# One reading of w1 between the second and the third pass of a decode gradient kernel

## The chip, the cores and the metric

The kernel runs on one core of one Trainium2 chip. The metric is the device time of one execution in microseconds (us). One execution was recorded by the hardware profiler, and all times of single instructions below are from that record.

## The reference, cut to what matters

A small network for one token is run forwards and backwards. Attention block A reads a cache of keys and values (4 groups, 65536 positions, 128 wide, bf16); block B is a dense layer, and both are applied twice with the same weights:

```python
def _B_ref(x, w1, b1, w2, b2):
    h = jnp.einsum("bsd,df->bsf", x, w1) + b1      # w1: 1024 x 3584
    r = jnp.where(h > 0, h, 0)
    return jnp.einsum("bsf,fd->bsd", r * r, w2) + b2

x = x + _A_ref(_layernorm(x), k_cache, v_cache, wq, wo)   # first A
x = x + _B_ref(_layernorm(x), w1, b1, w2, b2)             # first B
x = x + _A_ref(_layernorm(x), k_cache, v_cache, wq, wo)   # second A
x = x + _B_ref(_layernorm(x), w1, b1, w2, b2)             # second B
# returned: x and the gradients by x, k_cache, v_cache, wq, wo, w1, b1, w2, b2
```

With `n` the normalised input of the second B and `g` the incoming gradient, the part that matters here is `h = n w1 + b1`, then `dh = 2 relu(h) (g w2^T)`, then `dn = dh w1^T`. The first product needs columns of w1 as stationary operands, the last one needs w1 turned.

## The kernel before, in words

The kernel goes over the cache four times: pass 1 and pass 2 are the two attention blocks forwards, pass 3 and pass 4 are them backwards. Between passes stand dense stages for the projections, the layer normalisation and block B. This text is about the dense stage between pass 2 and pass 3.

All large loads go to one SBUF tile, `arena`, cut into 20 slots of 1 MB (128 partitions x 4096 bf16). A planner in Python (`Slot`, `take_one`, `take_pair`, `FREE`) decides while the program is built which slot each load takes. Eight of the slots hold softmax weights of the passes (planes), and seven hold blocks of V that pass 2 keeps for pass 3, already turned. So the dense stage has five slots. The loads are issued by SyncE in one queue in the order of the program (`kv8`, L352 for one slot and L357 for a pair; `slabs`, L449, for weights). A load into a slot waits until the last reader of its old content is done, and whatever stands behind it in the queue waits as well.

Within the passes the order of TensorE (PE), VectorE (DVE) and ScalarE (ACT) is as written. In the dense stages a scheduler may mix neighbouring steps when the program is built. Each engine then runs its own list in order.

The steps of the dense stage before:

- `g_wo`: the last group's rows of wo are multiplied with the attention output, 64 matmuls of 64 columns (`g_mv`, L506), and added to `x3` (L908). The two loads were issued during pass 2.
- `ln_fwd`: the layer normalisation, two tiny matmuls (L212), DVE steps (L221 to L234) and one square root on ACT (L229). It ends with `L4["nb"]`.
- `g_w1`: w1 is read as 8 slabs of 128 rows x 3584 columns (896 KB each). Each slab gives 28 matmuls of 18 columns (L506); `h` is complete after the last slab. `ffn_act` then makes relu, square and their bf16 form.
- L1659: `dh4`, the gradient by h, from `dg4` (made between pass 1 and 2) and relu(h).
- `Rows` with `mix=True`: w1 is read a second time in the same slabs. A piece of 8 blocks of a slab is either turned on PE (L669), copied from PSUM by DVE or ACT (`evac`, L164 and L161) and multiplied with `dh4` (L701), or multiplied and summed on DVE alone (L660). A cost model (`load`) chooses per piece.
- `fin_dx3`: `ln_bwd` (L239 to L249) and `dx3` (L1655).
- `Rows` with `inplace=True`: 1024 rows of wo (two loads of 1 MB) are turned on PE (L669, 64 transposes), copied back into their slots, and multiplied with `dx3` (L701, 64 matmuls). `dO_finish` (L933 to L947) makes of it what pass 3 needs first; L933 is the first instruction after the last of these matmuls.

Pass 3 (`attn_bwd3`) turns V (L1201), multiplies it with the output gradient (L1221), and 13 steps later multiplies blocks of K (L1246). The kept blocks of V go first, and the first blocks of K are loaded in the dense stage as its slots come free. In the background of pass 3, `g_dO` reads rows of wo for the next group (multiplied on DVE, L585).

Of the kernel before, what the change touches and what calls it, by code (L numbers as in the profile page):

```python
# [10 lines left out]
BF = mybir.dt.bfloat16  # L11
F32 = mybir.dt.float32
ACTF = mybir.ActivationFunctionType
ALU = mybir.AluOpType
# [6 lines left out]
def kernel(  # L21
# [66 lines left out]
    def ps_tr(shape=None, dtype=BF):  # L88
        return PS["pool"].tile(shape or [P, 8, P], dtype, name="ps_tr", tag="tr", bufs=2 if PS["pass4"] else 3)

    def ps_sc(shape, dtype=F32):
        return PS["pool"].tile(shape, dtype, name="ps_sc", tag="sc", bufs=1 if PS["pass4"] else 2)
# [122 lines left out]
    def ln_fwd(x, name):  # L215
        s = tmp.tile([P, 1], F32, name="ln_s")
        nc.vector.reduce_sum(out=s[:], in_=x[:], axis=AX.X)
        mean = bcast_sum(s[:], 1, mean=True)
        xc = tmp.tile([P, DC], F32, name="ln_xc")
        negmean = tmp.tile([P, 1], F32, name="ln_negmean")  # L220
        nc.vector.tensor_scalar(out=negmean[:], in0=mean[:], scalar1=-1.0, scalar2=None, op0=ALU.mult)  # L221
        nc.vector.tensor_scalar(out=xc[:], in0=x[:], scalar1=negmean[:, 0:1], scalar2=None, op0=ALU.add)
        sq = tmp.tile([P, DC], F32, name="ln_sq")
        ss = tmp.tile([P, 1], F32, name="ln_ss")
        nc.vector.tensor_tensor(out=sq[:], in0=xc[:], in1=xc[:], op=ALU.mult)
        nc.vector.reduce_sum(out=ss[:], in_=sq[:], axis=AX.X)
        var = bcast_sum(ss[:], 1, mean=True)
        rstd = vec.tile([P, 1], F32, name=name + "_rstd")
        nc.scalar.activation(out=rstd[:], in_=var[:], func=ACTF.Sqrt, bias=eps_t[:], scale=1.0)  # L229
        nc.vector.reciprocal(out=rstd[:], in_=rstd[:])  # L230
        n = vec.tile([P, DC], F32, name=name + "_n")
        nc.vector.tensor_scalar(out=n[:], in0=xc[:], scalar1=rstd[:, 0:1], scalar2=None, op0=ALU.mult)
        nb = vec.tile([P, DC], BF, name=name + "_nb")
        nc.vector.tensor_copy(out=nb[:], in_=n[:])  # L234
        return n, nb, rstd

    def ln_bwd(dn, n, rstd):
        st = tmp.tile([P, 2], F32, name="lnb_st")
        nc.vector.reduce_sum(out=st[:, 0:1], in_=dn, axis=AX.X)  # L239
        pr = tmp.tile([P, DC], F32, name="lnb_pr")  # L240
        nc.vector.tensor_tensor(out=pr[:], in0=dn, in1=n[:], op=ALU.mult)
        nc.vector.reduce_sum(out=st[:, 1:2], in_=pr[:], axis=AX.X)
        tot = bcast_sum(st[:], 2, mean=True)
        negm = tmp.tile([P, 2], F32, name="lnb_negm")
        nc.vector.tensor_scalar(out=negm[:], in0=tot[:], scalar1=-1.0, scalar2=None, op0=ALU.mult)
        t = tmp.tile([P, DC], F32, name="lnb_t")
        nc.vector.scalar_tensor_tensor(out=t[:], in0=n[:], scalar=negm[:, 1:2], in1=dn, op0=ALU.mult, op1=ALU.add)  # L247
        dx = tmp.tile([P, DC], F32, name="lnb_dx")
        nc.vector.tensor_scalar(out=dx[:], in0=t[:], scalar1=negm[:, 0:1], scalar2=rstd[:, 0:1], op0=ALU.add, op1=ALU.mult)  # L249
        return dx  # L250
# [175 lines left out]
    def rows_of(W):  # L426
        return W.rearrange("(kc p) n -> p kc n", p=P)
# [50 lines left out]
    def wo_slabs(g, ahead=1):  # L478
        v = rows_of(A_wo)
        return slabs("s_wo", lambda k, kn: v[:, g * R + k:g * R + k + kn, :], R, 4, 1024, ahead, True)  # L480
# [6 lines left out]
    def w1_slabs(ahead=1):  # L487
        v = rows_of(B_w1)
        return slabs("s_w1", lambda k, kn: v[:, k:k + kn, :], DC, 1, F, ahead)
# [109 lines left out]
    class Rows:  # L599
# [147 lines left out]
        def run(self):  # L747
            self.fill()
            first = self.queue[0][0] if self.queue else None
            while first is not None and first["inplace"] and self.queue and self.queue[0][0] is first:  # L750
                self.back()
            self.fill()
            while self.queue:
                self.back()
                self.fill()
# [150 lines left out]
    def g_wo(L, xacc, g, ps=ps_bg, it=None):  # L906
        def fin(p):
            nc.vector.tensor_tensor(out=xacc[:], in0=xacc[:], in1=p, op=ALU.add)  # L908
        if it is not None:
            yield from g_mv(it, R, 8, lambda kc: L["oTb"][:, g * R + kc:g * R + kc + 1], ps, fin)  # L910
            return
        each = tmp.tile([P, R, 8], BF, name="run_each", bufs=1)
        nc.vector.tensor_tensor(out=each[:, :, :], in0=L["oTb"][:, gsl(g)].unsqueeze(2).to_broadcast([P, R, 8]),
                                in1=eighth[:, :].unsqueeze(1).to_broadcast([P, R, 8]), op=ALU.mult)
        yield
        pt = ps_mv([P, R, 8])
        nc.tensor.matmul(pt[:, :, :].rearrange("p r k -> p (r k)"), lhsT=to_runs[:, :, :].rearrange("p a b -> p (a b)"),
                         rhs=each[:, :, :].rearrange("p r k -> p (r k)"), start=True, stop=True)
        yield
        own = tmp.tile([P, 8, R], F32, name="run_own", bufs=1)  # L920
        nc.vector.tensor_tensor(out=own[:, :, :], in0=pt[:, :, :].rearrange("p r k -> p k r"),
                                in1=M8[:, :].unsqueeze(1).to_broadcast([P, 8, R]), op=ALU.mult)
        oruns = tmp.tile([P, 8], F32, name="run_o")
        nc.vector.tensor_reduce(out=oruns[:], in_=own[:, :, :], axis=AX.X, op=ALU.add)
        orunb = tmp.tile([P, 8], BF, name="run_ob")
        nc.vector.tensor_copy(out=orunb[:], in_=oruns[:])
        yield
        yield from g_mv(wo_runs(g), R, 8, lambda kc: orunb[:, kc:kc + 1], ps, fin)


    def dO_finish(L, g):
        def fin(y):
            nc.vector.tensor_copy(out=L["dOT"][:, gsl(g)], in_=y)  # L933
            prod = tmp.tile([P, R], F32, name="dlt_prod")
            nc.vector.tensor_tensor(out=prod[:], in0=L["dOT"][:, gsl(g)], in1=L["oT"][:, gsl(g)], op=ALU.mult)
            yield
            pd = ps_mv([33, R], F32)
            nc.tensor.matmul(pd[:, :], lhsT=ones_f[:, 0:33], rhs=prod[:, :], start=True, stop=True)
            yield
            negd = tmp.tile([33, R], F32, name="negd")  # L940
            nc.vector.tensor_scalar(out=negd[:], in0=pd[:], scalar1=-1.0, scalar2=None, op0=ALU.mult)
            hi = tmp.tile([33, R], BF, name="negd_hi")
            nc.vector.tensor_copy(out=hi[:], in_=negd[:])
            lo = tmp.tile([33, R], BF, name="negd_lo")
            nc.vector.tensor_tensor(out=lo[:], in0=negd[:], in1=hi[:], op=ALU.subtract)
            nc.vector.tensor_copy(out=L["nd2"][0:1, gsl(g)], in_=hi[0:1, :])
            nc.vector.tensor_copy(out=L["nd2"][32:33, gsl(g)], in_=lo[32:33, :])  # L947
        return fin
# [619 lines left out]
    def g_w1(L, ps, pre=None, it=None):  # L1568
        def fin(p):
            L["r"], L["g"], L["gb"] = ffn_act(p, L["name"])  # L1570
        yield from g_mv(it or w1_slabs()[0], DC, FC, lambda kc: L["nb"][:, kc:kc + 1], ps, fin, pre=pre, cols=f_cols)
# [37 lines left out]
    L2["n"], L2["nb"], L2["rstd"] = ln_fwd(x1, "L2")  # L1609
    run(g_w1(L2, ps_mv))  # L1610
    x2 = vec.tile([P, DC], F32, name="x2")
    dg4 = vec.tile([P, FC], F32, name="dg4")
    rows = Rows(DENSE["pool"])

    def fin_dg4(y):
        nc.vector.tensor_copy(out=dg4[:], in_=y)
    dgjob = rows.job(FC, DC, lambda: gx[:], fin_dg4, mix=True, vbc=gxbc)

    def side(kc, slab):
# [23 lines left out]

    reset_load()
    dst = open_dense("dense23")
    run(g_wo(L3, x3, lastg[1], ps_mv, PRE["wo3"]))
    L4 = dict(name="L4")
    L4["n"], L4["nb"], L4["rstd"] = ln_fwd(x3, "L4")
    rows = Rows(DENSE["pool"])
    dh4 = vec.tile([P, FC], F32, name="dh4")  # L1650
    dx3 = vec.tile([P, DC], F32, name="dx3")

    def fin_dx3(y):
        dxn = ln_bwd(y, L4["n"], L4["rstd"])
        nc.vector.tensor_tensor(out=dx3[:], in0=gx[:], in1=dxn[:], op=ALU.add)  # L1655
    rows.add(w1_slabs()[0], DC, FC, lambda: dh4[:], fin_dx3, cols=f_cols, mix=True)
    rows.add(wo_slabs(firstg[2])[0], R, DC, lambda: dx3[:], dO_finish(L3, firstg[2]), inplace=True)
    run(g_w1(L4, ps_mv, pre=rows.fill))
    nc.vector.scalar_tensor_tensor(out=dh4[:], in0=dg4[:], scalar=2.0, in1=L4["r"][:], op0=ALU.mult, op1=ALU.mult)  # L1659
    rows.run()  # L1660
    dst.close()

# [143 lines left out]
```

## Time and profile before

| what | value |
|---|---|
| device time, three runs | 1979.23, 1986.36, 1986.77 us; median 1986.36 us |
| profiled execution | span 1985.4 us from first to last instruction; the median of the runs is 0.96 us above it |
| busy, share of the span | PE 81%, DVE 59%, ACT 53%, GpSimd 7% |
| HBM | 624.96 MB read, 165.69 MB written, 398 GB/s over the span |
| DMA issues of w1 in the whole kernel | 32 of 896 KB, 7.5 us median from issue to landing |
| granted PE clock, mean | 0.905 of full speed |
| `arena` loads of w1 in this dense stage | 16, issued from 739.9 to 791.9 us of the span |

How to read it: the share of busy time is an average over stages with different limits. In a window of the trace, "DMA share" is the mean busy share of the core's 16 DMA engines, and "PEclk" is the clock that was granted to PE, 1.00 being full speed. A PE row with "x64" is 64 matmuls in a row, so its length over 64 is the pace; PEld rows are the loads of the stationary operands that go with them. SPq rows are issues of loads.

### The profile page before, as it was taken

To read this page: it belongs to the slowest core of one execution; us is meant where nothing else is said; L and a number is where in the kernel's file an instruction comes from. 1 tells how busy PE (TensorE), PEld (TensorE's weight loads), DVE (VectorE), ACT (ScalarE), POOL (GpSimd) and SP (SyncE) were. 2 spreads that over 40 slices of the span, in tenths; PEclk is the share of its full clock that TensorE was granted. 3 is DMA by queue.
4 is the path that set the end of the run, shared out by engine and by line. 5 is a ranking of instruction groups with operands and counts; after the bars stand their busy time and mean duration, and the time that the engine had idled before them with its cause. 6 is when DMAs were issued, how large, how long until landed. Compare 5 with 4: busy or idle time off the path is not lost. (4 is left out here: it accounts for less than half of the span.)

```text
span 1985.4 us, 67093 instructions
## 1 busy us (share of the span) xinstructions
PE 1614.0 (81%) x30228; PEld 1317.7 (66%) x30228; DVE 1174.4 (59%) x2426; ACT 1043.6 (53%) x1608; POOL 142.6 (7%) x332
## 2 busy tenths in 40 slices
PE   6878787687877877787877888887889898788897
PEld 6878777677777877786776886554556465455554
DVE  5645455255555543544544566877687586758666
ACT  3444344154344453534453455766678586657666
POOL 0000000000000000000000001111111111111211
PEclk9999899699999997998989999999899798879978
DMA  9999999999999998899999988999999999999996
GB/s 389 423 422 422 423 425 400 394 400 420 425 419 424 425 405 310 359 421 420 421 422 421 411 304 307 406 425 404 397 424 424 425 425 411 361 424 424 425 377 256
DMA packets 101037, 794.98 MB, mean 400 GB/s; under 512 B 9472, under 2 KB 9486, under 8 KB 37134
## 3 DMA queue, kind: packets, MB, share of 16 engines
q1 hardware_dynamic: 76670, 624.99, 76.6%
q0 software_dynamic: 24080, 165.70, 20.1%
q8 instruction: 236, 3.87, 0.8%
q14 instruction: 51, 0.42, 0.1%
HBM read 624.96 MB, written 165.69 MB: 398 GB/s over the span
## 5 line engine op out<-in xcount | busy, mean ns | idle before, releaser
L164 DVE COPY kt<-ps_tr 128x1024 bf16<-128x1024 bf16 x724 | 497.4, 689 | 431.0 <-PE ps_tr L1009 248.5
L161 ACT CAST arena<-ps_gg 128x1024 bf16<-128x1024 f32 x457 | 446.0, 1013 | 226.7 <-PE ps_gg L1393 140.2
L1009 PE MATMUL ps_tr<-ident_b,arena 128*128 128x128 bf16 x3840 | 310.4, 226 | 44.7 <-DMA arena<-in_A_k_cache_dram 30.7
L164 DVE CAST arena<-ps_gg 128x1024 bf16<-128x1024 f32 (+2 forms) x186 | 222.5, 1196 | 113.4 <-PE ps_gg L1471 47.8
L161 ACT COPY kt<-ps_tr 128x1024 bf16<-128x1024 bf16 x164 | 171.1, 1047 | 191.6 <-PE ps_tr L1201 111.7
L1009 PEld LDWEIGHTS <-arena 128*128 128x128 bf16 x3840 | 234.5, 101 | 54.0 <-DMA arena<-in_A_k_cache_dram 33.6
L1111 PE MATMUL ps_acc<-arena 128*128 128x64 bf16 (+4 forms) x4096 | 206.1, 196 | 66.1 <-DMA arena<-in_A_v_cache_dram 53.7
L1393 PE MATMUL ps_gg<-GG,xt 64*128 64x512 bf16 x1024 | 215.2, 418 | 28.2 <-ACT arena L161 10.1
L1111 PEld LDWEIGHTS <-arena 128*128 128x128 bf16 x4096 | 160.0, 101 | 71.8 <-DMA arena<-in_A_v_cache_dram 57.5
L1092 ACT ACTIVATE arena<-S_sb,L_negm 128x128 bf16<-128x128 f32 x256 | 165.6, 1003 | 61.1 <-DVE L_negm L1077 61.1
L1027 PE MATMUL ps_sc<-L_qpad,kt 128*128 128x64 bf16 (+7 forms) x3584 | 183.6, 194 | 11.2 <-issue 6.4
L1201 PE MATMUL ps_tr<-ident_b,arena 128*128 128x128 bf16 x1920 | 156.2, 227 | 44.4 <-DMA arena<-in_A_v_cache_dram 43.0
L1321 PE MATMUL ps_tr<-ident_b,arena 128*128 128x128 bf16 x1824 | 180.5, 235 | 10.4 <-DMA arena<-in_A_v_cache_dram 8.3
L1321 PEld LDWEIGHTS <-arena 128*128 128x128 bf16 x1824 | 118.9, 104 | 67.7 <-issue 56.9
L1027 PEld LDWEIGHTS <-kt 128*128 128x128 bf16 x3584 | 153.7, 100 | 15.2 <-issue 6.6
L1201 PEld LDWEIGHTS <-arena 128*128 128x128 bf16 x1920 | 118.6, 102 | 49.4 <-DMA arena<-in_A_v_cache_dram 45.5
L1424 PEld LDWEIGHTS <-arena 128*128 128x128 bf16 x2048 | 94.6, 102 | 59.8 <-issue 42.9
L1092 ACT ACTIVATION_READ_ACCUMULATOR arena<-S_sb,L_negm 128x1 f32 x256 | 128.1, 500 | 0.0
L1352 PEld LDWEIGHTS <-kt 128*128 128x128 bf16 x1824 | 84.5, 103 | 51.6 <-issue 50.1
L1352 PE MATMUL ps_sc<-DOB,kt 128*128 128x64 bf16 (+3 forms) x1824 | 114.7, 200 | 0.0
L1246 PE MATMUL ps_acc<-dsT,arena 128*128 128x64 bf16 (+7 forms) x2048 | 103.4, 194 | 13.5 <-DMA arena<-in_A_k_cache_dram 9.8
L1393 PEld LDWEIGHTS <-xt 64*128 64x128 bf16 x1024 | 65.7, 94 | 71.5 <-issue 33.0
(292 smaller groups left out, 2196.2 us busy)
## 6 DMA issues: line engine op xcount, KB each, us to landing
arena<-in_A_k_cache_dram SPq DMA_DIRECT2D x86, 2048.0 KB, 21.1
arena<-in_A_v_cache_dram SPq DMA_DIRECT2D x83, 2048.0 KB, 21.1
out_dram<-arena POOLq DMA_DIRECT2D x149, 1024.0 KB, 13.5
arena<-in_A_v_cache_dram SPq DMA_DIRECT2D x76, 1024.0 KB, 17.3
arena<-in_A_k_cache_dram SPq DMA_DIRECT2D x76, 1024.0 KB, 16.3
arena<-in_B_w_dram SPq DMA_DIRECT2D x32, 896.0 KB, 7.5
arena<-in_A_wo_dram SPq DMA_DIRECT2D x22, 1024.0 KB, 19.4
arena<-in_A_wq_dram SPq DMA_DIRECT2D x20, 1024.0 KB, 24.4
```

Of the source, the lines that this page charges most:

```text
L161: nc.scalar.copy(out=out, in_=in_)
L164: nc.vector.tensor_copy(out=out, in_=in_)
L1009: nc.tensor.transpose(pt[:, i, :], kb8[:, i, :], ident_b[:, :])
L1027: nc.tensor.matmul(state["ps_s"][:, s:s + w, :].rearrange("p a b -> p (a b)"), lhsT=kt[:, i, :], rhs=L["qpad"][:, g, 0:w, :].rearrange("p ...
L1092: nc.scalar.activation(out=E(p, g, c0, SU)[:, :, h], in_=S[:, h, :], func=ACTF.Exp, bias=L["negm"][:, g, su, h:h + 1], scale=SCALE, accum_ ...
L1111: nc.tensor.matmul(ps_o[:, 0:w, :], lhsT=vb8[:, i, :], rhs=E(p, g, c, w), start=(c % SU == 0), stop=(c % SU == SU - 1), skip_group_check=True)
L1201: nc.tensor.transpose(pt[:, i, :], vb8[:, i, :], ident_b[:, :])
L1246: nc.tensor.matmul(ps_dq[:, 0:w, :].rearrange("p a b -> p (a b)"), lhsT=kb8[:, i, :], rhs=dsT[:, s:s + w, :].rearrange("p a b -> p (a b)") ...
L1321: nc.tensor.transpose(pt[:, i, :], vb8[:, i, :], ident_b[:, :])
L1352: nc.tensor.matmul(state["ps_dp"][:, s:s + w, :].rearrange("p a b -> p (a b)"), lhsT=vt[:, i, :], rhs=DOB[:, g, 0:w, :].rearrange("p a b - ...
L1393: nc.tensor.matmul(pg[:, 512 * h:512 * h + 512], lhsT=xt[64 * h:64 * h + 64, j1 // 8 + m, :], rhs=gg[64 * h:64 * h + 64, :, :].rearrange(" ...
L1424: nc.tensor.matmul(ps_dq[:, 0:w, :].rearrange("p a b -> p (a b)"), lhsT=kb8[:, i, :], rhs=X[:, s:s + w, :].rearrange("p a b -> p (a b)"), ...
```

## The change

w1 is read once in this stage, in 7 pieces of 512 columns (all 1024 rows, so 1024 runs of 1 KB, 1 MB per piece, one slot). Each piece is turned on PE (`ch_turn`, 32 transposes and 4 copies into `wt`, 8 buffers), multiplied forwards (`ch_fwd`, 32 matmuls of 64 columns, which makes 512 values of h and, since `dg4x2` is already doubled, of dh in two DVE instructions), and multiplied backwards from its turned form (`ch_bwd`, 32 matmuls of 64 columns into one accumulator `ps_dn`). The backward product of a piece comes one piece later than its forward product. The choice of DVE for some pieces, the broadcast of `dh4` over partitions and the second reading go away. The first piece is turned ahead of `g_wo`, the second ahead of the forward products. The turning of the wo rows is placed ahead of the last piece's backward product. The relu, square and bf16 forms of h are made at the end of the stage.

```diff
-    dg4 = vec.tile([P, FC], F32, name="dg4")
+    dg4x2 = vec.tile([P, FC], F32, name="dg4x2")
...
-        nc.vector.tensor_copy(out=dg4[:], in_=y)
+        nc.vector.tensor_scalar(out=dg4x2[:], in0=y, scalar1=2.0, scalar2=None, op0=ALU.mult)
...
-    run(g_wo(L3, x3, lastg[1], ps_mv, PRE["wo3"]))
-    L4["n"], L4["nb"], L4["rstd"] = ln_fwd(x3, "L4")
-    rows = Rows(DENSE["pool"])
...
-    rows.add(w1_slabs()[0], DC, FC, lambda: dh4[:], fin_dx3, cols=f_cols, mix=True)
-    rows.add(wo_slabs(firstg[2])[0], R, DC, lambda: dx3[:], dO_finish(L3, firstg[2]), inplace=True)
-    run(g_w1(L4, ps_mv, pre=rows.fill))
-    nc.vector.scalar_tensor_tensor(out=dh4[:], in0=dg4[:], scalar=2.0, in1=L4["r"][:], op0=ALU.mult, op1=ALU.mult)
+    def ch_load(s):
+        sl = Slot("s_w1c")
+        v = sl.t[:, :].rearrange("p (k n) -> p k n", n=512)
+        nc.sync.dma_start(out=v, in_=rows_of(B_w1)[:, :, 512 * s:512 * s + 512])
+        w1c[s] = (sl, v)
+    def ch_cols(s, kc, j):
+        return w1c[s][1][:, kc, bass.ds(j, P, step=4)]
+    def ch_turn(s):
+        for j in range(4):
+            pt = ps_tr()
+            for kc in range(DC):
+                nc.tensor.transpose(pt[:, kc, :], ch_cols(s, kc, j), ident_b[:, :])
+            wt = DENSE["pool"].tile([P, 8, P], BF, name="wt", tag="wt", bufs=8)
+            evac(wt[:, :, :], pt[:, :, :])
+            w1t[(s, j)] = wt
+    def ch_fwd(s):
+        ps = ps_sc([P, 4, 64])
+        for j in range(4):
+            for kc in range(DC):
+                nc.tensor.matmul(ps[:, j, :], lhsT=ch_cols(s, kc, j), rhs=L4["nb"][:, kc:kc + 1].to_broadcast([P, 64]),
+                                 start=kc == 0, stop=kc == DC - 1, skip_group_check=True)
+        c = slice(4 * s, 4 * s + 4)
+        nc.vector.tensor_tensor(out=h4[:, c], in0=ps[:, :, 0], in1=b1c[:, c], op=ALU.add)
+        nc.vector.scalar_tensor_tensor(out=dhb[:, c], in0=h4[:, c], scalar=0.0, in1=dg4x2[:, c], op0=ALU.max, op1=ALU.mult)
+    def ch_bwd(s, ps):
+        for j in range(4):
+            wt = w1t.pop((s, j))
+            for kc in range(DC):
+                nc.tensor.matmul(ps[:, kc, :], lhsT=wt[:, kc, :], rhs=dhb[:, 4 * s + j:4 * s + j + 1].to_broadcast([P, 64]),
+                                 start=s == 0 and j == 0 and kc == 0, stop=s == NCH - 1 and j == 3 and kc == DC - 1, skip_group_check=True)
+    rows = Rows(DENSE["pool"])
+    wo3b = wo_slabs(firstg[2])
+    ahead = 0
+    while ahead < 5 and FREE:
+        ch_load(ahead)
+        ahead += 1
+    ch_turn(0)
+    run(g_wo(L3, x3, lastg[1], ps_mv, PRE["wo3"]))
+    L4["n"], L4["nb"], L4["rstd"] = ln_fwd(x3, "L4")
+    ch_turn(1)
+    ps_dn = ps_bg([P, DC, 64])
+    for s in range(NCH):
+        ch_fwd(s)
+        ch_free(s)
+        if ahead < NCH:
+            ch_load(ahead)
+            ahead += 1
+        if s:
+            ch_bwd(s - 1, ps_dn)
+        if 0 < s < NCH - 1:
+            ch_turn(s + 1)
+    rows.add(wo3b[0], R, DC, lambda: dx3[:], dO_finish(L3, firstg[2]), inplace=True)
+    rows.fill()
+    ch_bwd(NCH - 1, ps_dn)
+    dxn4 = ln_bwd(ps_dn[:, :, 0], L4["n"], L4["rstd"])
+    nc.vector.tensor_tensor(out=dx3[:], in0=gx[:], in1=dxn4[:], op=ALU.add)
...
     rows.run()
```

More of the change, by code (lines that the diff above doesn't have):

```diff
@@ L1645 @@
     dst = open_dense("dense23")
-    run(g_wo(L3, x3, lastg[1], ps_mv, PRE["wo3"]))
+    NCH = F // 512
     L4 = dict(name="L4")
-    L4["n"], L4["nb"], L4["rstd"] = ln_fwd(x3, "L4")
-    rows = Rows(DENSE["pool"])
     dh4 = vec.tile([P, FC], F32, name="dh4")
     dx3 = vec.tile([P, DC], F32, name="dx3")
-    def fin_dx3(y):
-        dxn = ln_bwd(y, L4["n"], L4["rstd"])
-        nc.vector.tensor_tensor(out=dx3[:], in0=gx[:], in1=dxn[:], op=ALU.add)
-    rows.add(w1_slabs()[0], DC, FC, lambda: dh4[:], fin_dx3, cols=f_cols, mix=True)
@@ L1657 @@
-    rows.add(wo_slabs(firstg[2])[0], R, DC, lambda: dx3[:], dO_finish(L3, firstg[2]), inplace=True)
-    run(g_w1(L4, ps_mv, pre=rows.fill))
-    nc.vector.scalar_tensor_tensor(out=dh4[:], in0=dg4[:], scalar=2.0, in1=L4["r"][:], op0=ALU.mult, op1=ALU.mult)
+    h4 = tmp.tile([P, FC], F32, name="ffn_h")
+    dhb = vec.tile([P, FC], BF, name="dhb")
+    w1c, w1t, ph4 = {}, {}, {}
+    def ch_load(s):
[3 more added lines that the diff above has]
+        w1c[s] = (sl, v)
@@ new lines, in ch_free @@
+    def ch_free(s):
+        w1c.pop(s)[0].free()
+    def ch_bwd(s, ps):
[6 more added lines that the diff above has]
+    wo3b = wo_slabs(firstg[2])
@@ new lines @@
+    rows.add(wo3b[0], R, DC, lambda: dx3[:], dO_finish(L3, firstg[2]), inplace=True)
[3 more added lines that the diff above has]
+    nc.vector.tensor_tensor(out=dx3[:], in0=gx[:], in1=dxn4[:], op=ALU.add)
+    L4["r"] = vec.tile([P, FC], F32, name="L4_r")
+    nc.vector.tensor_scalar(out=L4["r"][:], in0=h4[:], scalar1=0.0, scalar2=None, op0=ALU.max)
+    L4["g"] = vec.tile([P, FC], F32, name="L4_g")
+    nc.vector.tensor_tensor(out=L4["g"][:], in0=L4["r"][:], in1=L4["r"][:], op=ALU.mult)
@@ L1660 @@
+    L4["gb"] = vec.tile([P, FC], BF, name="L4_gb")
+    nc.vector.tensor_copy(out=L4["gb"][:], in_=L4["g"][:])
+    nc.vector.tensor_tensor(out=dh4[:], in0=dg4x2[:], in1=L4["r"][:], op=ALU.mult)
     rows.run()
```

## The prediction

> **What bounds the kernel now.** I read the page first. Its chain of waits gives every share as 0%, so the bound is read from the DMA rows.
>
> ```profile
> span 1985.4 us, 67093 instructions
> ...
> DMA  9999999999999998899999988999999999999996
> ...
> q1 hardware_dynamic: 76670, 624.99, 76.6%
> q0 software_dynamic: 24080, 165.70, 20.1%
> ```
>
> The two data queues fill 96.7% of 16 engines' span. Outside the dense stages a microsecond is lost only where the DMA engines idle. So I looked at the stage in windows of 4 us; columns are window, length, busy time (and count) of PE, PEld, DVE, ACT, POOL, then granted clock, DMA share, rate.
>
> ```profile
> 752.00:756.00 4.00, 1.28 (x34) 1.19 (x35) 0.41 (x3) 0.00 (x0) 0.00 (x0) 1.00 0.52 215
> 756.00:760.00 4.00, 3.30 (x63) 3.22 (x63) 0.67 (x5) 1.51 (x2) 0.00 (x0) 0.57 0.54 162
> 764.00:768.00 4.00, 4.00 (x125) 4.00 (x124) 0.00 (x0) 0.00 (x0) 0.00 (x0) 0.50 0.79 278
> 776.00:780.00 4.00, 3.10 (x48) 2.92 (x48) 1.97 (x10) 0.00 (x0) 0.00 (x0) 0.50 1.02 421
> 784.00:788.00 4.00, 4.00 (x57) 3.32 (x56) 2.95 (x5) 2.99 (x5) 0.00 (x0) 0.90 0.31 126
> 820.00:824.00 4.00, 4.00 (x104) 3.58 (x100) 1.82 (x4) 1.01 (x1) 0.00 (x0) 1.00 0.36 143
> 824.00:828.00 4.00, 4.00 (x119) 3.64 (x117) 1.68 (x3) 2.74 (x5) 0.00 (x0) 1.00 0.41 102
> 836.00:840.00 4.00, 0.66 (x7) 0.66 (x8) 0.71 (x2) 2.54 (x6) 0.00 (x0) 0.80 1.01 430
> ```
>
> Seen here: the DMA engines idle whenever all five free slots are full and PE has not yet released one. In this stage the chain on PE, not the bytes, sets when loads can start; from 828 on the share is near 1 again. The forward loop runs at half clock and waits for w1 in between. The timeline (start, length, engine, line) gives the landmarks:
>
> ```profile
> 756.87 3.41 PE L506 MATMUL ps_mv<-L_oTb,arena 128*128 128x64 bf16 x64 [0.70 <-DVE L_oTb L1148]
> 763.59 4.81 PE L506 MATMUL ps_mv<-L_nb,arena 128*128 128x18 bf16 x140 [1.11 <-DVE L_nb L234]
> 778.06 2.92 PEld L669 LDWEIGHTS <-arena 128*128 128x128 bf16 x28
> 803.44 1.80 PEld L669 LDWEIGHTS <-arena 128*128 128x128 bf16 x32
> 807.40 2.15 PE L701 MATMUL ps_bg<-vcb,arena 128*128 128x64 bf16 x64
> 809.59 0.17 DVE L933 COPY L_dOT<-ps_bg 128x8 f32<-128x8 f32 x1 [0.82 <-PE ps_bg L701]
> 825.54 0.33 SPq L357 DMA_DIRECT2D arena<-in_A_k_cache_dram  x1
> 829.42 0.33 SPq L357 DMA_DIRECT2D arena<-in_A_v_cache_dram  x1
> ```
>
> Paces follow: a 64-column matmul takes 53 ns at half clock (3.41/64) and 33 ns at full clock (2.15/64); a transpose takes 104 ns (2.92/28) or 57 ns (1.80/32). The chain from 756.87 to 809.59 is 52.7 us: wo 3.4, normalisation 3.3, forward loop 13.4, gradient 1.1, second reading 25.5, tail 6.0.
>
> **Bytes removed.** Sixteen loads of 896 KB become seven of 1 MB: 14.68 MB become 7.34 MB. At the 424 GB/s of the passes this is 17.3 us of DMA time, the most that can be gained. It is gained only if idle does not grow; the chain decides how much.
>
> **The chain after, on PE.** Its order is that of the built program.
> 1. The first piece's 32 transposes stand after the 18th of the 64 wo matmuls. Its load takes the queue place of the first slab, which I put at 757 to 758.5 because the second and third landed at 758.7 and 760.5. Transposes at 1.8 us (full clock) to 3.3 us (half): I take 2.7, and 0.4 of waiting. With wo's 3.4: done at 763.4 instead of 760.3.
> 2. Normalisation 3.3 us, but 36 transposes stand on PE between its two matmuls and three copies of 0.69 us on DVE between its steps: +2.1. Forward starts at 768.8 instead of 763.6. So far 5.2 us lost.
> 3. Seven forward and seven backward products of 32 matmuls at 33 ns: 14.8 us. Transposes left by then, 8 + 4x32 = 136 at 57 ns: 7.7 us. Only three PSUM buffers take transposes, so a fourth group waits for a copy, 0.3 us for each of five pieces: 1.5 us. Sum 24.0, to 792.8. The DVE steps between forward and backward (two of about 0.2 us) are hidden by the piece of delay; without that cover they would cost some 0.6 us a piece.
> 4. Turning wo, 64 at 57 ns: 3.7, to 796.5. It is no longer hidden by the normalisation backwards, which before ran under it.
> 5. Normalisation backwards without the mask steps, 2.8 (804.41 to 807.3 before); wo matmuls 2.15 and 0.2 to L933. It ends at 801.6 instead of 809.6: 8.0 us gained.
>
> **Queue order.** SyncE's list behind the stage is unchanged in its loads; only slots differ. Pieces 4 and 5 wait for wo's slots and pieces 6 and 7 for the first two forward products; behind them in SyncE's queue stand the wo rows and then K for pass 3. The piece issued last leaves at about 771 and is needed after 785; alone, a slab landed in 4.5 us, so this wait is hidden. The 1 KB runs are in no row of before: from below 0, from above by the 2 KB runs of wo.
>
> ```profile
> DMA to landing us min/median/max: 4.5/7.6/17.8
> DMA to landing us min/median/max: 5.8/18.9/33.5
> ```
>
> The first line is w1 in this stage, the second all loads of wo. A 1 MB load of 2 KB runs needs 5.8 at best, 4.5 scaled to 1 MB is 5.1; twice the packets again would add 1.4 us a piece. On the path lies only the first piece: 0 to 1.5 us, and I take the 0.4 of step 1, nearer to nothing because the queue is full of 8 KB runs at that time.
>
> **Start of pass 3.** In the windows from 820 to 828 the DMA idles 8 x (1 - 0.385) = 4.9 us, until the pair of K at 825.54. In the changed order that pair reuses slots that the first block of K frees, 74 PE instructions earlier, at 41 ns (8 in 0.33 us in pass 3) 3.0 us; the following V pair no longer waits for a slot of wo rows. PE starves at 836 for this V. Gain 3.0, bounds 0 and 4.9.
>
> **Sum.** 8.0 + 3.0 = 11.0 us. Span 1985.4 - 11.0 = 1974.4, and 1.0 us around it as before (median 1986.36): 1975.4 us. Pass 3 and later are a shift, for their lists are the same.
>
> [...] The trace: from 763.6 PE was busy without a gap for 4.8 us, and the clock stayed at 0.50; the wo matmuls of 64 columns before it raised it to 0.92 (window 760 to 764). So busy time alone does not raise it; 18-column matmuls do not, 64-column ones did. [...]
>
> **Rivals.**
> - Clock stays at half (slower). After 768.8 the 200 transposes cost 47 ns more and 512 matmuls 20 ns more: 9.4 + 10.2 us; ahead of it 36 transposes and the rest of wo about 2.9. That is +22.5: 1997.9 us. It decides once about half of the stretch from 769 to 800 is at 0.5 (mean granted clock under 0.75). For it: 776 to 780 at 0.50. Against: the new work is 64 and 128 columns wide without gaps. Chance 0.09.
> - The gain is hidden. Order and waits on PSUM eat the chain's gain, or pass 3 is held by another slot: 8.0 less 2 (late piece), 1.5 (copies), 1.2 (cold wo), and nothing at 820: 3.3 gained, 1983 us. Chance 0.24.
> - Idle does not grow at all: 17.3 us, 1969 us. Against it: the loads still wait for PE. Chance 0.07.
> - The forecast, 7 to 15 us gained: 0.60.
>
> **Range and chances.** Unknowns go from 3.3 to 15.5 gained (step 1 by 1.1 the other way, no PSUM waits, all idle filled). The runs of before lie 7.5 us apart, so I widen to 1967 and 1985. The clock rival is left out. About 0.5%, 9.9 us, is what a measurement of this kernel can tell from no change: 1976.4 is the line, close to the forecast. Faster: 0.8 of the forecast's 0.60 and the 0.07, 0.55. Within: the rest of the forecast and the hidden case, 0.36. Slower: 0.09.
>
> **What would show it.** After: L933's first copy at about 802 instead of 809.6; forward start near 769; granted clock 1.0 from about 765 to 800; DMA idle between 770 and 800 clearly larger than before; the first K pair some 11 us before 825.5; no PE wait on w1 after the first piece. A forward start past 772, a clock of 0.5 past 775, or a piece of over 4.8 us on PE would make it wrong.

## The result, and the profile after

The changed kernel takes 1959.97 us (median of 5 runs, 1959.29 to 1961.16) against 1981.2 us of the kernel before in the same comparison (5 runs, 1978.91 to 1986.77). The ratio is 0.9883, with the interval [0.9872, 0.9893]. Four more runs in a later comparison gave 0.9869 [0.9852, 0.9886]. The medians of the kernel before lay between 1981.2 and 1986.0 us in the four comparisons of this study; where a ratio is turned into microseconds below, it is multiplied by 1984. The change thus gains 23 to 26 us by these ratios; the two medians of the first comparison lie 21.2 us apart. Predicted were 11, and the range ended at 1967.

First the page of the changed kernel, with the lines that answer to those of the kernel before, and its rate in 40 slices of the span:

```profile
span 1957.5 us, 67228 instructions
...
DMA  9999999999999999899999987999999999999996
GB/s 395 426 427 427 426 427 410 400 400 425 428 426 427 428 412 315 328 425 428 426 423 420 403 319 283 415 425 403 384 424 424 426 424 411 370 424 424 424 405 259
...
q1 hardware_dynamic: 81646, 617.65, 76.7%
q0 software_dynamic: 24080, 165.70, 20.3%
```

The same rate row of the kernel before:

```profile
GB/s 389 423 422 422 423 425 400 394 400 420 425 419 424 425 405 310 359 421 420 421 422 421 411 304 307 406 425 404 397 424 424 425 425 411 361 424 424 425 377 256
```

The two data queues moved 7.34 MB less, as planned. The second thing to see is the start of the two rows: 426 to 427 GB/s where it was 422 to 425. That is pass 1, ahead of every changed instruction, and the DMA digit is 9 in both. The loads there have become faster without any change to them.

Next the timeline of the changed kernel (start, length, engine, line) at the landmarks of the prediction; L1669 turns a piece, L1679 is the forward product, L701 multiplies the rows of wo:

```profile
748.28 0.72 PE L506 MATMUL ps_mv<-L_oTb,arena 128*128 128x64 bf16 x18 [0.71 <-DVE L_oTb L1148]
748.84 2.00 PE L1669 MATMUL ps_tr<-ident_b,arena 128*128 128x128 bf16 x32
750.67 1.59 PE L506 MATMUL ps_mv<-L_oTb,arena 128*128 128x64 bf16 x46
757.42 2.29 PE L1679 MATMUL ps_sc<-L_nb,arena 128*128 128x64 bf16 x64 [0.77 <-DVE L_nb L234]
771.49 2.00 PE L1669 MATMUL ps_tr<-ident_b,arena 128*128 128x128 bf16 x32
786.22 3.48 PE L701 MATMUL ps_bg<-vcb,arena 128*128 128x64 bf16 x64 [1.24 <-DVE vcb L542]
789.74 0.17 DVE L933 COPY L_dOT<-ps_bg 128x8 f32<-128x8 f32 x1 [3.58 <-PE ps_bg L701]
802.39 0.33 SPq L357 DMA_DIRECT2D arena<-in_A_k_cache_dram  x1
```

The first wo matmul, the start of the chain, stands at 748.28 instead of 756.87: 8.6 us were already gained when the stage began. From there to L933 it is 41.5 us instead of 52.7, so 11.3 us were gained in the stage. From L933 to the first K pair of pass 3 it is 12.65 us instead of 15.95.

The stage in windows of 4 us (the last three columns are granted clock, DMA share, GB/s):

```profile
748.00:752.00 4.00, 3.72 (x93) 3.72 (x93) 1.70 (x6) 2.16 (x3) 0.00 (x0) 1.00 0.80 279
756.00:760.00 4.00, 3.23 (x91) 3.12 (x89) 1.11 (x7) 0.69 (x3) 0.00 (x0) 1.00 0.78 259
764.00:768.00 4.00, 4.00 (x102) 4.00 (x101) 2.30 (x5) 1.05 (x2) 0.00 (x0) 1.00 1.07 399
776.00:780.00 4.00, 4.00 (x101) 3.94 (x99) 2.94 (x11) 1.04 (x2) 0.00 (x0) 1.00 0.83 270
784.00:788.00 4.00, 2.23 (x42) 2.08 (x40) 1.41 (x8) 0.00 (x0) 0.00 (x0) 0.81 0.00 0
800.00:804.00 4.00, 4.00 (x105) 3.62 (x101) 1.97 (x4) 1.01 (x1) 0.00 (x0) 1.00 0.50 164
```

Up to 784 PE is busy with small gaps and at full clock from the first piece on; from 784 to 788 it is busy for 2.23 of 4 us and the granted clock falls to 0.81. The DMA engines still idle when no slot is free: from 784 to 788 they move nothing at all.

### The profile page after: what moved, and what is told of

Its sections match the earlier page's. It is cut to its first block, busy times and chain, and to the rows that moved or that the text cites. A ratio compares the mean times of both kernels' runs of the same rounds, so it can differ in the third digit from the quotient of the medians.

```text
span 1957.5 us, 67228 instructions
## 1 busy us (share of the span) xinstructions
PE 1609.0 (82%) x30319; PEld 1313.9 (67%) x30319; DVE 1169.7 (60%) x2421; ACT 1039.4 (53%) x1600; POOL 142.1 (7%) x321
## 5 line engine op out<-in xcount | busy, mean ns | idle before, releaser
L1424 PEld LDWEIGHTS <-arena 128*128 128x128 bf16 x2048 | 95.7, 103 | 60.3 <-issue 42.7
L1424 PE MATMUL ps_acc<-X,arena 128*128 128x64 bf16 (+3 forms) x1536 | 102.1, 200 | 12.5 <-DMA arena<-in_A_k_cache_dram 12.5
```

What stands on the lines that cost most here:

```text
L1424: nc.tensor.matmul(ps_dq[:, 0:w, :].rearrange("p a b -> p (a b)"), lhsT=kb8[:, i, :], rhs=X[:, s:s + w, :].rearrange("p a b -> p (a b)"), ...
```

## The experiments

The question was where the 8.6 us ahead of the stage come from, and whether the chain inside it is worth what was summed. The built programs give a candidate. The change adds and removes small vectors in the pool that stands ahead of `arena` in SBUF, so that `arena` starts 64 bytes later in every partition: at 48896 (a multiple of 256) instead of 48832 (192 above one). The experiments with a padding move it, and the tiles that lie behind it, without touching any work; their lines stand two lower in the code.

**e1, the kernel before, unchanged, once more** (chance between executions):

> The kernel before, unchanged, profiled once more, to learn how much of the 27.9 us between the two profiled spans belongs to the one record of before. Run theory (the rate of the loads in the passes differs from run to run, by chance): this span may lie anywhere from 1958 to 1986, and its first wo matmul after pass 2 nearer to 748 than to 757 us. Address theory (the change moved the start of the arena in SBUF from 48832 to 48896 bytes, that is from 192 to 0 beyond a multiple of 256, and each load packet is slower at the old address): the passes are as slow as in the first record, first wo matmul at 755 to 758 us, 16 KB packets at a median of 613 ns against 611 after the change. Under both the dense stage from the first wo matmul to L933 takes 51 to 53 us.

Measured: 1979.53 us in one run, span 1977.7 us. The first wo matmul stood at 756.7 us, and half of the 16 KB packets took 613 ns or more. The time at which a given amount of the large loads had landed agreed with the first record within 0.5 us up to 731 us. Chance between executions does not make pass 1 and 2 faster by 8 us.

**e2 and e11, the kernel before with 64 bytes more:**

```diff
+    pad_t = vec.tile([P, 32], BF, name="pad_t")
+    nc.gpsimd.memset(pad_t[:], 0.0)
```

> The kernel before with an unused tile of 64 bytes per partition ahead of the other vectors, so that the arena starts at 48896 as in the changed kernel; nothing else differs. Address theory: passes at the rate of the changed kernel, about 10.7 us less before the end of pass 3, a ratio to before of 0.995 to 0.997. Run theory: ratio 0.999 to 1.001.

> The kernel before with 64 bytes more ahead of the arena, once more. Address theory: ratio 0.9936 (12 to 14 us), so that 8 to 11 us are left for the change itself. Run chance alone: 1.000.

Measured: 0.9936 [0.9913, 0.9959] and, in the later comparison, 0.9934 [0.9917, 0.9952]. Thus 64 bytes of padding that nobody reads are worth 12.7 and 13.1 us, somewhat more than e2's expectation of 10.7.

**e3, the changed kernel moved back to the old offset** (192 bytes more):

```diff
+    pad_t = vec.tile([P, 96], BF, name="pad_t")
+    nc.gpsimd.memset(pad_t[:], 0.0)
```

> The changed kernel with an unused tile of 192 bytes per partition, so that the arena starts 192 bytes beyond a multiple of 256 again, as before. Address theory: about 1967 us, a ratio to before of 0.992 to 0.993, that is the 14.4 us of stage and pass start alone. Run theory: 1960 us, 0.988 to 0.989.

Measured: 0.9956 [0.9938, 0.9973], 1974.57 us and not the expected 1967. At the old offset the change is worth 8.7 us, less than the 14.4 that the first two records had suggested.

**e7 and e8, two more offsets.** e7 is the kernel before with 320 bytes more (49152, a multiple of 512 too), e8 the changed kernel with 128 bytes more (49024, 128 above a multiple of 256):

> The kernel before with 320 bytes more per partition ahead of the arena, which then starts at 49152 (a multiple of 256 and of 512 bytes) instead of 48832. Address theory in its form 'a slot that starts on a multiple of 256 bytes is loaded faster': as with 64 bytes more, ratio 0.9936 (0.991 to 0.996), 16 KB packets of 611 ns in the first three passes. If it were 64 bytes as such, or one lucky address: ratio 1.000. If multiples of 512 matter too: below 0.990.

> The changed kernel with 128 bytes more per partition ahead of the arena, which then starts at 49024 (128 above a multiple of 256). Address theory, any start off a multiple of 256 costs the same extra: as with 192 bytes more, ratio 0.9956, 16 KB packets of 613 ns. If only offsets that are not multiples of 128 cost: ratio 0.988. If the cost grows with the distance from the multiple: between.

Measured: e7 0.9938 [0.9914, 0.9961], as with 64 bytes; e8 0.9947 [0.9929, 0.9965], as with 192 bytes. So it is not one lucky address; a multiple of 512 brings nothing further, and by the times of the kernel 128 off cannot be told from 192 off. Windows of pass 2 and pass 3 show it, first the kernel before, then e2:

```profile
520.00:660.00 140.00, 109.25 (x2609) 104.19 (x2610) 72.42 (x171) 56.07 (x138) 0.00 (x0) 0.95 1.01 423
880.00:1020.00 140.00, 112.06 (x2410) 103.13 (x2407) 68.98 (x132) 65.42 (x91) 0.00 (x0) 0.88 1.01 420
```

```profile
520.00:660.00 140.00, 111.83 (x2602) 106.75 (x2598) 71.47 (x160) 58.97 (x142) 0.00 (x0) 0.93 1.01 427
880.00:1020.00 140.00, 108.60 (x2383) 100.20 (x2379) 68.27 (x131) 66.93 (x94) 0.00 (x0) 0.91 1.01 425
```

And the changed kernel at the two bad offsets, e3 and then e8:

```profile
520.00:660.00 140.00, 110.48 (x2618) 105.67 (x2618) 72.42 (x169) 56.63 (x139) 0.00 (x0) 0.94 1.01 423
880.00:1020.00 140.00, 108.36 (x2323) 99.81 (x2322) 67.12 (x129) 66.37 (x94) 0.00 (x0) 0.89 1.01 420
```

```profile
520.00:660.00 140.00, 109.90 (x2623) 105.16 (x2619) 73.30 (x172) 56.03 (x137) 0.00 (x0) 0.95 1.01 422
880.00:1020.00 140.00, 110.04 (x2391) 101.56 (x2388) 68.16 (x130) 66.46 (x93) 0.00 (x0) 0.90 1.00 417
```

The DMA share is full in all eight lines; only the rate differs, and it follows the offset and not the kernel. The single packets in the records say the same. Between 60 and 700 us of the span, the packets of 2 KB, 8 KB and 16 KB in the load queue took on average 87.8, 318.5 and 619.4 ns in the kernel before and 84.3, 314.7 and 615.6 ns in the changed one; e2 and e7 stand with the latter (16 KB: 615.5 and 615.4), e3 and e8 with the former (619.3 and 618.9). Times the number of packets (7168, 2944 and 13369 in the kernel before), and spread over 16 engines, these differences make some 5.5 us (an estimate) of the 640, most of what the passes gained. In pass 4, where stores run in the other queue, packets of 8 KB show no such difference (medians of 309 ns in all).

**e4, the bytes alone.** The kernel before, where the second reading of w1 loads only 512 of the 3584 columns of each slab (the rest of the slot keeps what it held), 6.3 MB less, with all other work as it was:

```diff
-            nc.sync.dma_start(out=v, in_=load(k, kn))
+            nc.sync.dma_start(out=v if part is None else v[:, :, 0:part], in_=load(k, kn))
...
-    rows.add(w1_slabs()[0], DC, FC, lambda: dh4[:], fin_dx3, cols=f_cols, mix=True)
+    rows.add(w1_part()[0], DC, FC, lambda: dh4[:], fin_dx3, cols=f_cols, mix=True)
```

> The kernel before, but its second reading of w1 loads only 512 of the 3584 columns of each slab; all instructions on PE, DVE and ACT stay, the other columns are what the slot held, so the input gradient of the second B is another one. 6.3 MB fewer are read, 14.8 us at 424 GB/s. Bytes theory (in the dense stage, too, the gain is the bytes that are not read): 14 us less, ratio 0.993. Chain theory (PE's chain from pass 2 to pass 3 sets when slots come free, the bytes fall into idle DMA time): 0 to 5 us less, ratio 0.9975 to 1.000; the little there is comes from shorter waits for slabs between 776 and 800 us.

Measured: 1.0016 [1.0003, 1.0029], none of the 14 us, and if anything a little slower than either theory said. Its windows inside the second reading show where the bytes went:

```profile
776.00:780.00 4.00, 4.00 (x58) 3.73 (x57) 2.71 (x9) 3.10 (x4) 0.00 (x0) 0.75 0.19 63
780.00:784.00 4.00, 4.00 (x78) 3.60 (x77) 4.00 (x8) 2.94 (x5) 0.00 (x0) 1.00 0.11 33
```

The DMA share falls to 0.11 to 0.19 while PE is busy all the time: the time of the bytes turned into idle time. Between the landing of 275 and of 310 MB of large loads (the stage and what lies next to it) the DMA engines were busy for 122.6 us instead of 136.3 in the first record of before, and idle for 25.7 instead of 14.2. Taking away these bytes without shortening the chain gained nothing.

**e5 and e12, the first piece turned behind the normalisation:**

```diff
-    ch_turn(0)
     run(g_wo(L3, x3, lastg[1], ps_mv, PRE["wo3"]))
     L4["n"], L4["nb"], L4["rstd"] = ln_fwd(x3, "L4")
+    ch_turn(0)
     ch_turn(1)
```

> The changed kernel with the first piece's 32 transposes moved from between the wo matmuls to behind the normalisation; all else as changed. Chain theory: the 64 wo matmuls and the normalisation run undisturbed (2.2 us at full clock or 3.4 at half, then 3.3), then 64 transposes at 57 ns, 1.1 us of them beside the last steps of the normalisation: the forward products start 8.1 to 9.3 us after the first wo matmul, against 9.1 in the changed kernel. Time 1959 to 1961 us, ratio 0.988 to 0.989. Rival (the early transposes keep the clock up through wo and the normalisation): the first wo matmuls and transposes run at half clock, start 10.5 to 12.5 us after the first wo matmul, ratio 0.990 or more. Address theory: no part in this, since the arena starts where it does in the changed kernel.

> The first piece's transposes behind the normalisation, once more: its first measurement was 0.9859 although its stage took 2 us longer in the trace. Chain theory: same as the changed kernel or 1 to 3 us slower (0.9883 to 0.990); the first value was spread. Rival (a later start of the pieces is better for pass 3 and 4): 0.986 again, 4 us below the changed kernel in the same call.

Measured: 0.9859 [0.984, 0.9877], then 0.9887 [0.9869, 0.9904]. In the traces the forward products start 10.3 and 9.4 us after the first wo matmul (the changed kernel: 9.1 in the first record). The first value did not come back; the two runs together say that the place of these transposes cannot be told from no change.

**e6, the last backward product ahead of the turning of wo:**

```diff
+    ch_bwd(NCH - 1, ps_dn)
     rows.add(wo3b[0], R, DC, lambda: dx3[:], dO_finish(L3, firstg[2]), inplace=True)
     rows.fill()
-    ch_bwd(NCH - 1, ps_dn)
```

> The changed kernel with the last backward product moved ahead of the 64 transposes of wo, so that the normalisation backwards runs on DVE beside them. Chain theory: the 4.5 us between the last backward product and L933's copy, in which PE was busy for little and fell to 54 ns a matmul, shrink: transposes 3.6 us from the product's end, then 64 matmuls at 33 ns; L933 comes 2 to 3.5 us earlier counted from the first wo matmul (38 to 39.5 us instead of 41.5). Time 1956.5 to 1958 us, ratio 0.9865 to 0.9875. Bytes theory (DMA sets the time there): no change, 0.988 to 0.989, since the loads and their order are the same.

Measured: 0.9883 [0.9863, 0.9903], no gain, and 41.7 us from the first wo matmul to L933. The expectation was wrong. The timeline shows why:

```profile
778.83 2.17 PE L1693 MATMUL ps_bg<-dhb,wt 128*128 128x64 bf16 x64
784.97 0.34 PE L212 MATMUL ps_mv<-lnb_st,onesd_f 128*128 128x2 f32 x2
787.12 3.17 PE L701 MATMUL ps_bg<-vcb,arena 128*128 128x64 bf16 x64 [1.82 <-DVE vcb L542]
```

The product ends at 781.0, but the matmul that the normalisation backwards needs (L212) stands on PE behind all 64 transposes, at 784.97. After it PE has nothing left but to wait 1.82 us, and the wo matmuls run at 50 ns each, as in the first record of the changed kernel (54 ns).

**e9, half of the turning behind the last product,** the copies of that half on ACT, and the other forms of h made after the wo matmuls:

```diff
-    rows.fill()
+    rows.stop = 4
+    rows.feed = rows.fronts()
+    next(rows.feed)
     ch_bwd(NCH - 1, ps_dn)
...
+    add_load(dve=20.0)
+    rows.fill()
+    add_load(dve=-20.0)
+    rows.run()
```

> The changed kernel with 32 of the 64 transposes of wo moved behind the last backward product, their copies all on ACT, and the steps that only make h's other forms moved behind the wo matmuls. Chain theory: the product is ready 1.8 us earlier, its normalisation runs on DVE beside the 32 transposes, whose queue on PE no longer holds the normalisation's own matmul back by more than 10 of them, and PE does not fall to half clock: wo matmuls at 33 to 40 ns. L933's copy comes 38.5 to 40 us after the first wo matmul instead of 41.5. Time 1.5 to 3 us below the changed kernel in the same call, ratio to before 0.001 to 0.0015 lower. Rival (gains in this stage are taken back by pass 4): stage as above, times the same.

Measured: 0.989 [0.9869, 0.9911]; the unedited changed kernel had 0.9869 [0.9852, 0.9886] beside it. The tail did become shorter: from the first transpose of wo to L933 it took 7.7 us (783.98 to 791.7) instead of 10.4 (779.32 to 789.74). Some of that is the clock: in e3, where the last wo matmuls ran at full clock, the old order took 9.1 us (788.77 to 797.87). And the timeline of this execution begins with the stage at half clock (L705 is the line that was L701):

```profile
748.38 1.12 PE L506 MATMUL ps_mv<-L_oTb,arena 128*128 128x64 bf16 x18 [0.70 <-DVE L_oTb L1152]
752.70 2.31 PE L506 MATMUL ps_mv<-L_oTb,arena 128*128 128x64 bf16 x46
789.10 1.92 PE L705 MATMUL ps_bg<-vcb,arena 128*128 128x64 bf16 x56
```

46 matmuls took 2.31 us (50 ns each) here and 1.59 us (35 ns) in the first record of the changed kernel. The forward products started 11.8 us after the first wo matmul instead of 9.1, and L933 came 43.3 us after it, not the expected 38.5 to 40. In this record the one ate the other; whether the 1.4 to 2.7 us of tail reach the end of the kernel stays open, since the intervals of the times are wider than that.

**e10, the changed kernel once more:**

> The changed kernel once more, beside the kernel before with 64 bytes more ahead of the arena, on the same chip. Address theory and chain theory together: ratio 0.988 as first measured; against the moved kernel before 0.9947 (8 to 11 us, all from the stage and the start of pass 3). Rival (the two effects overlap, as the loads set the time in both): 0.991 or more against before.

Measured: 0.9869 [0.9852, 0.9886]. With e11 in the same comparison, 0.0065 or 12.9 us are left for the change at equal offset. No version beat the changed kernel measurably.

## Why the prediction was wrong

**The split.** At equal offset the change is worth 0.0053 (changed against e2), 0.0065 (e10 against e11), 0.0044 (e3 against before) and 0.0053 (e8 against before) of the time: 10.5, 12.9, 8.7 and 10.5 us, mean 10.7, each with an uncertainty of 3.5 to 5 us by the intervals of its ratios (the first joins two comparisons). The prediction's sum was 11.0, so the gain of the edited lines came as forecast, as far as 3.5 to 5 us can tell. The offset is worth 12.3 to 14.5 us: 12.7 (e2), 12.3 (e7), 13.1 (e11) on the kernel before, and 14.5 and 12.7 (e3 and e8 against the first comparison) on the changed one.

**The step that failed** is the last sentence of "Sum": "Pass 3 and later are a shift, for their lists are the same", together with the silent assumption behind "Span 1985.4 - 11.0" that passes 1 and 2 stay as they are. The lists are indeed the same, but the destination of every large load had moved by 64 bytes. The sum put this term at nothing; it measured 12.3 to 14.5 us. The packet records show where the time sits. They give the time in which the named MB of the load queue (packets of 8 KB and more, 553.6 MB in every kernel) landed:

| offset above a multiple of 256 | kernels | 5 to 275 MB, pass 1, pass 2 and the stage between | 275 to 310 MB, this stage | 310 to 410 MB, pass 3 | 410 to 550 MB, pass 4 |
|---|---|---|---|---|---|
| 192 | before, e1 | 709.6, 710.0 us | 150.6, 148.2 | 254.8, 255.0 | 766.6, 765.6 |
| 0 | before moved: e2, e7, e11 | 702.3, 700.9, 702.6 | 150.7, 149.8, 153.7 | 252.3, 252.3, 252.4 | 769.0, 772.5, 772.3 |
| 0 | changed, e10 | 702.1, 701.6 | 135.4, 137.7 | 252.2, 253.3 | 769.6, 770.5 |
| 192, 128 | changed moved: e3, e8 | 709.4, 708.8 | 140.3, 143.0 | 255.2, 256.2 | 768.2, 773.6 |

The first and third columns go by the offset alone: 7.5 us and 2.8 us. The second goes by the kernel: 150.6 against 139.1 us on average, 11.5 us for the change with the start of pass 3. (At offset 0 the difference is 14.8 us, off it 7.8; so few records do not say whether that is more than scatter.) In this column the DMA engines were busy for 136.4 us on average before and 122.9 after, 13.5 less, and idle for 14.1 and 16.2. The fourth column scatters by 8 us, and the rest behind it, from 550 MB to the end of the span, tends the other way. Both together, from 410 MB to the end, take 843.7 to 849.4 us in the four records off a multiple of 256 and 842.0 to 847.1 in the five on one, on average 3.2 us apart. With the 10.3 of the first and third columns this is about the 12 to 14 us of the offset, but the last 3.2 lie within the scatter.

**The steps of the chain, one by one.**

- Step 1 (wo with the first piece, 6.5 us): 4.0 in the first record and in e3, 5.3 in e10, 6.6 in e8 and e9. The half clock of the kernel before, 53 ns a matmul, was taken as given for this place. In both kernels it is there in some executions and not in others: e4, with the PE work of the kernel before, took 2.15 us for the 64 matmuls. The load of the first piece cost no wait.
- Step 2 (normalisation 3.3 + 2.1 us): 5.1, from 752.31 to 757.42. The forward products started 9.1 us after the first wo matmul against 11.9 in the sum; e8 and e9, at half clock, had 11.7 and 11.8.
- Steps 3 to 5 (768.8 to 801.6, so 32.8 us from the forward start to L933): 32.3 us (757.42 to 789.74). The rivals' clock at half did not come: the rows from 756 to 780 stand at 1.00, and 32 transposes took 2.00 us. The end took longer than summed, the wo matmuls: 3.48 us instead of 2.15. PE was idle for most of the normalisation backwards (busy for 2.23 of 4 us from 784 to 788), and the granted clock was 0.81 and 0.76 in the windows from 784 to 792. The hidden rival had it in its list (1.2 us, "cold wo"); shorter steps ahead of it, among them 2.15 us for the normalisation backwards instead of 2.8, paid for it. This price, too, differs between executions: with the same wait ahead of them the 64 matmuls took 2.82 us in e10, 2.90 in e8 and 2.16 in e3 (L703 there). In the five records of the kernel before, where PE had transposes to do in that place, they took 2.15 each time.
- Stage, over all records: 52.7, 50.1, 51.7, 52.3 and 54.3 us in the kernels before (first record, e1, e2, e7, e11), mean 52.2; 41.5, 41.8, 45.3 and 42.3 in the changed ones (first record, e3, e8, e10), mean 42.7. Gained 9.5, summed 8.0.
- Start of pass 3 (3.0 us): from L933 to the K pair 16.3 us on average before and 14.1 after (same records), 2.1 gained; 3.3 in the first pair of records.

The row of e3 for the last wo matmuls, to set beside the 3.48 us above:

```profile
795.67 2.16 PE L703 MATMUL ps_bg<-vcb,arena 128*128 128x64 bf16 x64 [1.25 <-DVE vcb L544]
```

**The rivals.** The full gain of the bytes (1969 us) gave a time nearer to the result, but by luck: it held no term for the offset either, and e4 shows that the bytes bring nothing without a shorter chain. In part it was right: the forecast implied that idle time grows by 6.3 us (17.3 less 11.0), and it grew by 2.1 on average (14.1 to 16.2), while the loads saved 13.5 us and not 17.3. The rival that the clock stays at half and the one that the gain is hidden did not come.

**The range** was made from the unknowns inside the stage and from the scatter of the runs. It held no term for what lies outside the edited lines, and its lower end was 7 us above the result.

## What to carry to other kernels

When an edit adds or removes a tile, compare the start addresses of the big load buffers in the two built programs as well as the order of instructions; here 64 bytes weighed as much as the whole rewrite. Put the buffer that all loads go to on a multiple of 256 bytes, which was worth 12.3 to 13.1 us to the kernel before (e7, e2, e11), before measuring anything else, and compare two versions at the same offset: at 192 above a multiple this change showed 0.9956 (e3) instead of 0.9883. In a stage where the loads wait for slots, price the chain that frees them, not the bytes: 6.3 MB fewer gave 1.0016 in e4.

## What the runs showed of the hardware

- Loads into slots that start 128 or 192 bytes above a multiple of 256 were slower here than into slots on one (64 off was not tried): 3.4 to 3.8 ns more per packet on average, for 2 KB and for 16 KB (87.8 against 84.3, 619.4 against 615.6 ns), 422 to 423 against 427 GB/s in pass 2, and about 13 us of 1984. In pass 4 no difference was seen (8 KB packets: medians of 309 ns). The times of e3 and e8 cannot tell 192 off from 128 off (0.9956 [0.9938, 0.9973] and 0.9947 [0.9929, 0.9965]), and the packets show little difference: 16 KB packets took 3.4 ns more than on a multiple in e8 and 3.8 in e3. What makes these packets slower is shown by no run.
- The clock at the start of the stage differs between executions of one kernel: the first 18 wo matmuls took 0.72 us in the first record of the changed kernel and 1.12 us in e10, with nearly the same idle stretch ahead of them (waits of 1.51 and 1.73 us for V); e8 was at half clock after only 1.26 us of that wait, e3 at full clock after 1.24. The records of the granted clock give one thing that goes with it: in each of the 14 records all changes of the granted clock (88 to 106 of them; 95 in the first record of the kernel before, 91 in that of the changed one) lie within 4 ns on one grid of 3.413 us. Where the wo matmuls began 0.35 to 1.02 us after a grid point, in seven records (0.35 in the first of the kernel before), the first 18 took 1.12 us; where they began 1.82 to 2.76 us after one, in five (2.76 in the first of the changed kernel), 0.72; the two between 2.97 and 3.13 lie between, at 0.83 and 0.94. The 1.3 to 2.7 us that hang on it here are a spread for the range, not a term of the sum.
- In the kernel before, the wo matmuls of 64 columns were on PE for 3.06 us of the grid step from 756.52 to 759.93, and the clock rose to full at its end. The 18-column matmuls of the forward loop were on PE for 3.17 us of the step from 763.34 to 766.76, and the clock stayed at 0.50 until 783.82. So in this record the prediction's reading stands that a busy PE alone did not raise the clock.
